# Moving element-wise sums from GpSimd to VectorE and giving the scatters a queue of their own, in a spectral filter followed by an eight-expert layer

## The chip, the core and the metric

The kernel runs on one core of a Trainium2 chip. The core has five engines, each with an instruction queue of its own that is worked off strictly in order: TensorE (PE in the profile; its weight loads are PEld), VectorE (DVE), ScalarE (ACT), GpSimd (POOL) and SyncE (SP, which here only issues DMA transfers). An instruction that must wait for another engine holds everything behind it in its own queue. The metric is the device time of one execution in microseconds (us). Nine executions of the kernel before gave a median of 1690.8 us (1688.98 to 1697.55).

## What is computed

Eight sequences of 2496 tokens with 256 channels are filtered in the frequency domain. Then each of the 19968 tokens goes to the one of eight experts for which its gate logit is largest, and the expert's output is scaled with the gate's probability.

```python
X = np.fft.rfft(x, axis=1)                      # x: (8, 2496, 256)
y = np.fft.irfft(X * (filt_r + 1j * filt_i)[None], n=2496, axis=1)
x = y.reshape(19968, 256)
logits = x @ w_gate                             # (19968, 8)
expert_idx = np.argmax(logits, axis=1)
gate_w = softmax(logits)[arange, expert_idx]
for e in range(8):                              # the rows of expert e
    h = np.maximum(x_e @ w1[e], 0.0)            # 256 -> 1024
    y_e = h @ w2[e]                             # 1024 -> 256
return gate_w[:, None] * y                      # float32 throughout
```

## The kernel before

**The filter, batch by batch.** The length 2496 = 39 x 64 is split into a 39-point and a 64-point transform, both done as matrix products, so that a batch goes through four stages: a (39 points, `stage_a`, L389), b (64 points and the filter, `stage_b`, L403), c (64 points back, `stage_c`, L432) and d (39 points back, `stage_d`, L451). Stages a and d run over six column chunks of four (the last of two) columns, b and c over five quarters of the frequencies. Between a and b, and between c and d, the data goes through DRAM (`zd`, `ud`), because rows and columns change places. All loads of x, z and u use one ring of seven buffers (`fin`). The first batch (`first_a`, `turn_z`, `first_c`, `turn_u`) stays on the chip.

Two kinds of sums concern us. `add_x` (L375) turns a chunk of x into sums `xs` (L382) and differences, written over the loaded tile (L383); stage a multiplies both. It runs on VectorE for batches 0 to 2 (`EARLY = 3`) and on GpSimd for batches 3 to 7. `xs` has two buffers. In `stage_b`, batches 0 to 2 keep the two products with the filter apart, and stage c accumulates both on TensorE. From batch 3 on, VectorE makes ys (L423), ScalarE copies the other parts in eight pieces of 32 partitions (L425), VectorE multiplies them (L426), and a sum of 128x1024 (L427) on GpSimd joins the two, for which stage c (L440) waits.

**Routing.** `turn_y` and `logits` make the gate logits; `route` (L569) then works on groups of eight columns (three groups per batch: 8, 8 and 6): some twenty small VectorE instructions find expert, gate and row for each token, with two small matrix products (L608, L609) for the ranks. Last, one indirect DMA per column, issued by GpSimd (L667, the "scatters"), writes 117 tokens to `rows`, a buffer in DRAM sorted by expert. The tiles `yo` that hold the tokens (six buffers) come free when their scatters have landed. `tile_map` (L685) works out which expert tiles a batch makes ready.

**The experts** run over tiles of 512, 256 or 128 rows: `rows_in` loads a tile (`xg`, by SyncE), `weights` loads w1 and w2, `turn_x` transposes (L798), `hidden` is the first product (L805) with a relu on ScalarE or VectorE, `result` the second (L819) with the gate, and GpSimd scatters the result to the output (L825).

**What sets the order.** The order of instructions on PE, DVE, ACT and SP is written by a loop at the end of the kernel (L988 to L1015). It takes steps from two lists: `STEPS` (the filter: fixed order, each with a TensorE cost) and `experts()`. Each turn of the loop emits one step, adds its TensorE cost to a planned clock `now`, and then calls `flush` (stores made in the turn before are issued), `more_loads` (fills the ring), up to four times `side`, and `prefetch` (rows and weights). A load counts as landed when `now` has passed its due time (`when`), 6 or 7 us after its issue. `free["v"]`, `free["s"]` and `free["p"]` are the planned times at which VectorE, ScalarE and GpSimd come free; `either` chooses by them whether VectorE or ScalarE copies a result out of PSUM.

`side` advances a queue `sides` of generators: `route` of each group of columns and, after a batch, `tile_map`. A generator is advanced one `yield` at a time, and the next one starts only when the one before has ended. The scatters are the last part of `route`; each `yield "pool"` stops the queue until GpSimd's planned time is within 1.5 us of `now`. Between the first part of `route` and its matrix products ten empty turns are let pass (L604). The count `held_y` of tiles in use falls by a group's tiles when its last scatter has been emitted; at six the filter's steps that need one are halted.

Of the kernel before, what the change touches and what calls it, by code (L numbers as in the profile page):

```python
# [14 lines left out]
ALU = mybir.AluOpType  # L15
# [21 lines left out]
NG = 2 * NI  # L37
# [117 lines left out]
def kernel(  # L155
# [18 lines left out]
    nc = tc.nc  # L174
# [94 lines left out]
    def pool(start, n):  # L269

        free["p"] = max(free["p"], start) + 1.3 * n
        return free["p"]
# [3 lines left out]
    EARLY = 3  # L276
# [98 lines left out]
    def add_x(b, c):  # L375

        m = CH[c][1] // 2
        xt = ins["x", b, c]
        xs = xss[b, c] = sb.tile([TP, 2, D], F32, tag="xs", name="xs", bufs=2)
        lo, hi_ = xt[:TP, :m], xt[:TP, m:2 * m]  # L380
        eng = nc.vector if b < EARLY else nc.gpsimd
        eng.tensor_tensor(xs[:, :m], lo, hi_, op=ALU.add)  # L382
        eng.tensor_tensor(hi_, lo, hi_, op=ALU.subtract)  # L383
        if b < EARLY:
            free["v"] = max(free["v"], now[0]) + 1.4
        else:
            free["p"] = max(free["p"], now[0]) + 2.6

    def stage_a(b, c):  # L389
        m = CH[c][1] // 2  # L390
# [12 lines left out]
    def stage_b(b, q):  # L403
        zi = outs.pop(("zi", q)) if b == 0 else ins.pop(("z", b, q))

        po = [bank(), bank()]
        for e in range(2):
            for o in range(2):
                rows = slice(o * HP, (o + 1) * HP)
                mm(po[o][e * HP:(e + 1) * HP, :], lhsT=tbs[rows, :], rhs=zi[rows, 2 * e:2 * e + 2, :], start=True, stop=True)  # L410

        ys = outs["y", b, q] = sb.tile([P, 2, 2 * D], F32, tag="ys", name="ys", bufs=2)
        yw = sb.tile([P, 2, 2 * D], F32, tag="yw", name="yw", bufs=2)
        if b < EARLY:

            for o in range(2):
                for y, h in ((ys, hr), (yw, hi)):
                    nc.vector.tensor_mul(y[:, o], po[o], h[:, q, 2 * o:2 * o + 2].rearrange("p j d -> p (j d)"))
            outs["w", b, q] = yw
            free["v"] = max(free["v"], now[0]) + 2.8  # L420
            return
        for o in range(2):
            nc.vector.tensor_mul(ys[:, o], po[o], hr[:, q, 2 * o:2 * o + 2].rearrange("p j d -> p (j d)"))  # L423
            for r in range(0, P, HB):
                nc.scalar.copy(out=yw[r:r + HB, o], in_=po[o][r ^ HB:(r ^ HB) + HB])  # L425
        nc.vector.tensor_mul(yw, yw, hi[:, q].rearrange("p (o j) d -> p o (j d)", o=2))  # L426
        nc.gpsimd.tensor_tensor(ys, ys, yw, op=ALU.add)  # L427
        free["s"] = max(free["s"], now[0]) + 4.7
        free["v"] = max(free["v"], now[0]) + 2.6
        free["p"] = max(free["p"], now[0]) + 2.5  # L430

    def stage_c(b, q):  # L432
        parts = [outs.pop((y, b, q)) for y in ("yw" if b < EARLY else "y")]
# [132 lines left out]
    scatters, rows_at, held_y = {}, {}, [0]  # L566


    def route(b, g):  # L569
        t0 = 8 * g  # L570
        w = min(8, NG - t0)
# [29 lines left out]
        nc.vector.tensor_reduce(sd, ex, axis=AX.X, op=ALU.add)  # L601
        yield

        for _ in range(10):  # L604
            yield
        rk = psr.tile([P, 2, E * NG], F32, tag="rk", name="rk")
        oef = oe.rearrange("p e t -> p (e t)")
        mm(rk[:TP, 0, :E * w], lhsT=tri, rhs=oef, start=True, stop=True)  # L608
# [7 lines left out]
        yos = [outs.pop(("o", b, c)) for c in range(2 * g, min(2 * g + 2, len(CH)))]  # L616
        for c, yo in enumerate(yos):
            n = min(4, w - 4 * c)
# [31 lines left out]
        rows = []  # L650
        for t in range(w):
            m = (HB - NB * (NI - 1)) * N1 if t0 + t >= NG - 2 else TP
            rows.append((row[:m, t:t + 1], yos[t // 4][:m, t % 4, :]))
        if b == B - 1 and t0 + w == NG:
# [8 lines left out]
            nc.vector.memset(fill.bitcast(I32)[:, D:D + 8], N)  # L663
            rows += [(pad[:, e:e + 1], fill) for e in range(E)]
        pool(now[0] + 2.0, 0)
        for t, (at, what) in enumerate(rows):
            sc = nc.gpsimd.indirect_dma_start(  # L667
                out=rowsd,
                out_offset=bass.IndirectOffsetOnAxis(ap=at, axis=0),
                in_=what,  # L670
                in_offset=None,
            )

            tc.declare_no_dep(sc.ins, group="scatter", reason="rows of their own")
            tc.declare_no_dep(sc.ins, group="listed", reason="rows of their own")
            tc.add_to_no_dep_group("scatter", sc.ins)
            scatters.setdefault(b, []).append(sc.ins.name)
            pool(now[0], 1)
            yield "pool"
        held_y[0] -= len(yos)  # L680
        if t0 + w == NG:
            rows_at[b] = free["p"] + 4.0


# [61 lines left out]
    work, idt, gts, xgs, xts, w1t, w2t, hs = [], {}, {}, {}, {}, {}, {}, {}  # L746
# [5 lines left out]
    late = {}  # L752

    def rows_in(i):

        n, e, r, b = work[i]
        r0 = nc.sync.value_load(r, min_val=0, max_val=TR - n * P)
        xg = xgs[i] = pools["moe"].tile([P, 4, DR], F32, tag="xg", name="xg")
        ld = nc.sync.dma_start(
            out=xg[:, :n], in_=rowsd[bass.ds(r0, n * P), :].rearrange("(p i) c -> p i c", i=n)  # L760
        )
        tc.add_to_no_dep_group("listed", ld.ins)
        for name in scatters.pop(b, ()):
# [68 lines left out]
        )  # L832


    sides = []

    def slot(k):

# [75 lines left out]
            if n:  # L914
                yield from tile_map(b, rows, n, rows == P)

    held = [None]

    def side():

        while sides and not (held[0] and free["p"] > now[0] + 1.5):
            try:
                held[0] = next(sides[0])

                free["v"] = max(free["v"], now[0]) + 0.3
                return
            except StopIteration:
                sides.pop(0)
                held[0] = None


    got = {"x": 0, "w1": 0, "w2": 0}
    used = {"x": 0, "w1": 0, "w2": 0}
    when = {}

    def prefetch():

        i = got["x"]
        if i < len(work) and rows_at[work[i][3]] <= now[0] and i - used["x"] < 2:
            rows_in(i)  # L940
            when["x", i] = now[0] + 6.0
            got["x"] += 1
        for what in ("w1", "w2"):
            h = got[what]
            if h < 2 * len(work) and rows_at[work[h // 2][3]] <= now[0] and (
                    h - used[what] < (3 if h < 2 * SHORT else 8)):
                weights(h, what == "w2")
                when[what, h] = now[0] + 7.0
                got[what] += 1
# [29 lines left out]
    with tc.manual_schedule(  # L979
        engines={mybir.EngineType.PE, mybir.EngineType.DVE, mybir.EngineType.Activation, mybir.EngineType.SP}  # L980
    ):
        nc.sync.dma_start(out=tas, in_=ta)
        more_loads()
        make_constants()
        fs, es = iter(STEPS), experts()
        credit = 0.0
        f, e = next(fs), next(es)
        while f or e:  # L988
            asked = e and e[2] in when

            halt = f and f[2] and f[2][0] in "uy" and held_y[0] == 6
            if e and asked and (not f and not sides or when[e[2]] <= now[0] and (credit > 0.0 or not f or halt)):
                e[0]()
                now[0] += e[1]
                credit -= e[1]
                e = next(es, None)
            elif f and not halt and (not f[2] or f[2] == "y" or f[2] in ins):
                f[1]()
                now[0] += f[3]
                credit = (credit if asked else 0.0) + share() * f[3]  # L1000
                left_t[0] -= f[3]
                f = next(fs, None)
            else:
                now[0] += 1.0
            flush()
            more_loads()
            for _ in range(4):
                side()
            if not f and not sides and not late:
                fft.close()  # L1010
                tail = ctx.enter_context(tc.tile_pool(name="tail", bufs=1))
                late["w1"] = ctx.enter_context(tc.tile_pool(name="w1b", bufs=8))
                late["n"] = 0
                late["w2s"] = tail.tile([P, E, FT, D], F32, name="w2s")
            prefetch()  # L1015
# [31 lines left out]
```

## Time and profile before

One profiled execution took 1690.43 us, of which 1688.7 us are its span (first to last instruction); 1.7 us lie around it.

| stretch of the span, us | PE busy | granted clock of PE | DVE busy | ACT busy | POOL busy | DMA share |
|---|---|---|---|---|---|---|
| 100 to 301.6 | 146.51 | 0.80 | 101.25 | 80.89 | 92.93 | 0.75 |
| 301.6 to 550 | 229.43 | 0.96 | 97.41 | 100.89 | 114.86 | 0.70 |
| 550 to 1200 | 627.95 | 0.99 | 161.75 | 215.16 | 195.29 | 0.48 |
| 1200 to 1689 | 482.50 | 0.99 | 20.68 | 150.26 | 68.50 | 0.51 |
| whole span | 1572.5 | 0.962 | 438.4 | 594.0 | 487.5 | |

The granted clock is the share of its full clock that TensorE got in the records of that stretch; a busy engine at a low clock does less. The DMA share is the mean busy share of the core's 16 DMA engines. At 301.6 us the first run of expert products without filter work between them begins; from about 1200 us on there are experts alone.

Instructions of the program as built, before and after, by engine: PE 4269 and 4269, DVE 1482 and 1532, ACT 1319 and 1354, POOL 458 and 373, SP 1928 and 1928.

### The profile page before, as it was taken

What the parts mean: (1) busy time and instruction counts of PE and PEld (TensorE: products, weight loads), DVE (VectorE), ACT (ScalarE), POOL (GpSimd) and SP (SyncE); (2) the same over time, 40 slices, a digit from 0 to 9 for tenths busy, and PEclk for the clock granted to TensorE, in tenths of its full rate; (3) what the DMA queues carried; (4) which work ended last, traced back from release to release, by engine and by line L of the source; (5) the groups of instructions that cost most, each with busy time, mean ns of one, the idle gap of its engine ahead of it and who ended that gap; (6) DMA issues with size and microseconds to landing.
All of it is one profiled execution on the core that took longest, in us unless ns stands there. A gap on an engine that the chain in (4) does not pass through costs nothing.

```text
span 1688.7 us, 22545 instructions
## 1 busy us (share of the span) xinstructions
PE 1572.5 (93%) x7218; PEld 1064.7 (63%) x7218; DVE 438.4 (26%) x1480; ACT 594.0 (35%) x1317; POOL 487.5 (29%) x453
## 2 busy tenths in 40 slices
PE   7987775899898999999979999999999999999998
PEld 5633442585444665557626666666666668889997
DVE  5564355124354115112244122112200000000000
ACT  4533444225453325232354323223222222333333
POOL 2034453442455235203234132133311111111111
PEclk9988786999999999999989999999999999999999
DMA  8579765578686357435374373343444446565661
GB/s 312 150 198 292 237 188 176 176 230 243 189 232 193 131 172 208 148 101 163 98 190 141 120 201 111 105 128 121 141 151 140 155 134 217 185 211 175 181 184 49
DMA packets 132325, 290.39 MB, mean 172 GB/s; under 512 B 21103, under 2 KB 62096, under 8 KB 132209
## 3 DMA queue, kind: packets, MB, share of 16 engines
q1 hardware_dynamic: 112993, 245.63, 48.5%
q0 software_dynamic: 19216, 43.33, 7.5%
q8 instruction: 59, 0.97, 0.2%
q14 instruction: 57, 0.47, 0.1%
HBM read 208.88 MB, written 80.90 MB: 172 GB/s over the span
## 4 chain that ended last, share of the span: by engine, by line
PE 82%; DVE 5%; issue 4%; DMA 3%; ACT 3%; POOL 2%; SPq 1%; POOLq 0%; DVEq 0%; ACTq 0%
PE bank L819 33%; PE bank L805 32%; PE bank L462 3%; PE bank L396 3%; ACT yw L425 2%; PE bank L798 2%; PE bank L410 2%; PE lt L551 2%; PE bank L537 1%; PE bank L440 1%; DMA fin<-in_x_dram 1%; PE bank L513 1%; POOL rows L667 1%; PE bank L489 1%; DMA xg<-rows 0%
## 5 line engine op out<-in xcount | busy, mean ns | idle before, releaser
L805 PE MATMUL bank<-xT,w1t 128*128 128x512 f32 (+2 forms) x2080 | 595.4, 440 | 14.0 <-issue 10.5
L819 PE MATMUL bank<-w2t,hT 128*128 128x256 f32 x2240 | 501.4, 382 | 5.7 <-issue 4.1
L805 PEld LDWEIGHTS bank<-xT,w1t 128*128 128x128 f32 x2080 | 340.6, 193 | 237.0 <-issue 203.2
L819 PEld LDWEIGHTS bank<-w2t,hT 128*128 128x128 f32 x2240 | 423.1, 191 | 74.6 <-issue 14.3
L825 POOL DMA_INDIRECT out_dram<-ys,idt x163 | 160.7, 986 | 773.6 <-ACT ys L824 443.9
L809 ACT ACTIVATE hT<-bank 128x512 f32<-128x512 f32 (+2 forms) x499 | 216.4, 435 | 327.4 <-PE bank L805 313.3
L667 POOL DMA_INDIRECT rows<-yo,row x176 | 177.6, 1009 | 236.1 <-DVE cnt L648 93.9
L824 ACT ACTIVATE ys<-bank,gts 128x256 f32<-128x256 f32 x156 | 73.6, 474 | 483.8 <-PE bank L819 420.0
L267 DVE COPY xT<-bank 128x512 f32<-128x512 f32 (+2 forms) x58 | 27.7, 477 | 540.0 <-PE bank L798 430.5
L425 ACT COPY yw<-bank 32x512 f32<-32x512 f32 x200 | 115.2, 576 | 52.3 <-DVE ys L423 41.7
L427 POOL TENSOR_TENSOR ys<-ys,yw 128x1024 f32<-128x1024 f32 x25 | 58.8, 2351 | 137.2 <-DVE yw L426 113.7
L819 PE MATMUL bank<-w2s,hT 128*128 x368 | 83.2, 379 | 0.0
L462 PE MATMUL bank<-fin,tds 120*117 120x512 f32 (+1 forms) x154 | 78.2, 627 | 1.3 <-ACT yw L425 1.3
L819 PEld LDWEIGHTS bank<-w2s,hT 128*128 128x128 f32 x368 | 68.1, 190 | 8.3
L396 PE MATMUL bank<-xs,tas 117*120 117x512 f32 (+1 forms) x84 | 45.2, 622 | 27.8 <-issue 12.3
L440 PE MATMUL bank<-ys,tcs 64*64 64x512 f32 x280 | 43.6, 676 | 17.5 <-POOL ys L427 17.4
L426 DVE TENSOR_TENSOR yw<-yw,hi 128x1024 f32<-128x1024 f32 x25 | 30.9, 1234 | 104.3 <-ACT yw L425 87.6
L466 DVE TENSOR_TENSOR yo<-bank,even 117x256 f32<-117x256 f32 x88 | 37.1, 422 | 78.5 <-ACT even L465 67.4
L537 PEld LDWEIGHTS bank<-ident,yo 117*128 117x128 f32 x352 | 40.5, 148 | 24.0 <-issue 16.7
L798 PEld LDWEIGHTS bank<-ident,xg 128*128 128x128 f32 x326 | 39.2, 143 | 23.0 <-issue 20.6
L537 PE MATMUL bank<-ident,yo 117*128 117x117 f32 x352 | 47.5, 278 | 6.2 <-ACT yw L425 2.8
L798 PE MATMUL bank<-ident,xg 128*128 128x128 f32 x326 | 47.4, 277 | 4.8 <-DMA xg<-rows 4.3
(140 smaller groups left out, 1105.2 us busy)
## 6 DMA issues: line engine op xcount, KB each, us to landing
w1t<-in_moe_w_dram SPq DMA_DIRECT2D x130, 512.0 KB
w2t<-in_moe_w_dram SPq DMA_DIRECT2D x84, 512.0 KB
fin<-in_x_dram SPq DMA_DIRECT2D x40, 512.0 KB
fin<-zd SPq DMA_DIRECT2D x140, 128.0 KB
ud<-uo SPq DMA_DIRECT2D x140, 128.0 KB
zd<-zo SPq DMA_DIRECT2D x70, 240.0 KB
fin<-ud SPq DMA_DIRECT2D x70, 240.0 KB
xg<-rows SPq DMA_DIRECT2D x28, 544.0 KB
```

The lines of the kernel that those rows point to most:

```text
L396: mm(p, lhsT=tas, rhs=v, start=True, stop=True)
L425: nc.scalar.copy(out=yw[r:r + HB, o], in_=po[o][r ^ HB:(r ^ HB) + HB])
L440: mm(pe[e][o * HP:(o + 1) * HP, :], lhsT=tcs[rows, o, i, :], rhs=y[rows, o, :], start=(i == 0), stop=(i == len(parts) - 1))
L462: mm(p[:TP, :], lhsT=tds[:k, :], rhs=uv[:, i], start=True, stop=True)
L537: nc.tensor.transpose(pt[:, 2 * i + dh, :TP], yo[:, j + i, dh * P:(dh + 1) * P], ident[:TP, :TP])
L667: sc = nc.gpsimd.indirect_dma_start(out=rowsd, out_offset=bass.IndirectOffsetOnAxis(ap=at, axis=0), in_=what, in_offset=None,)
L798: nc.tensor.transpose(pt[:, j, :], xg[:, j, dh * P:(dh + 1) * P], ident)
L805: mm(p[:, :m], lhsT=w1t[2 * i + k // FH2][:, dh, k % FH2 * P:(k % FH2 + 1) * P], rhs=xts[i][:, dh, :m], start=(dh == 0), stop=(dh == DH - 1))
L809: lambda: nc.scalar.activation(hT[:, :m], p[:, :m], AF.Relu))
L819: mm(p[:, :D], lhsT=hs[i][k][:, j * P:(j + 1) * P], rhs=w2, start=(k == 0), stop=(k == FT - 1))
L824: lambda: nc.scalar.activation(ys, p[:, :D], AF.Copy, scale=gate))
L825: nc.gpsimd.indirect_dma_start(out=out, out_offset=bass.IndirectOffsetOnAxis(ap=idt[i].bitcast(U32)[:, j, :], axis=0), in_=ys, in_offset=None,
```

## The change

1. `add_x` and the sum in `stage_b` run on VectorE in all batches. GpSimd keeps the scatters (and the constants at the start).
2. The scatters leave `route` for a generator of their own, `scatter`, in a queue `scats` beside `sides`; `scatter_on` advances it once per turn while GpSimd's planned time is within 1.5 us. The next group's routing need not wait for the scatters of the group before. `held_y` falls tile by tile, with every fourth scatter.
3. `side` takes a step whenever VectorE's planned time is at most 1 us ahead of `now`, and books 0.45 us for it (0.3 before). The ten empty turns become six that are marked "wait" and book nothing.
4. After each step the planned clock `now` is moved up to at least 3 us before VectorE's and ScalarE's planned times. `prefetch` counts a batch's rows as not ready (`rows_at.get`) while its scatters are still to be emitted.

```diff
 def add_x(b, c):
-        eng = nc.vector if b < EARLY else nc.gpsimd
-        eng.tensor_tensor(xs[:, :m], lo, hi_, op=ALU.add)
-        eng.tensor_tensor(hi_, lo, hi_, op=ALU.subtract)
-        if b < EARLY:
-            free["v"] = max(free["v"], now[0]) + 1.4
-        else:
-            free["p"] = max(free["p"], now[0]) + 2.6
+        nc.vector.tensor_tensor(xs[:, :m], lo, hi_, op=ALU.add)
+        nc.vector.tensor_tensor(hi_, lo, hi_, op=ALU.subtract)
+        free["v"] = max(free["v"], now[0]) + 1.4
 def stage_b(b, q):
-        nc.gpsimd.tensor_tensor(ys, ys, yw, op=ALU.add)
+        nc.vector.tensor_tensor(ys, ys, yw, op=ALU.add)
-        free["v"] = max(free["v"], now[0]) + 2.6
-        free["p"] = max(free["p"], now[0]) + 2.5
+        free["v"] = max(free["v"], now[0]) + 3.9
 def route(b, g):
-        for _ in range(10):
-            yield
+        for _ in range(6):
+            yield "wait"
...
         pool(now[0] + 2.0, 0)
+        scats.append(scatter(b, rows, len(yos), t0 + w == NG))
+
+    def scatter(b, rows, n, last):
         for t, (at, what) in enumerate(rows):
             sc = nc.gpsimd.indirect_dma_start(
...
             pool(now[0], 1)
-            yield "pool"
-        held_y[0] -= len(yos)
-        if t0 + w == NG:
+            if t % 4 == 3 and t // 4 < n or t == len(rows) - 1 and n > len(rows) // 4:
+                held_y[0] -= 1
+            yield
+        if last:
             rows_at[b] = free["p"] + 4.0
 def side():
-        while sides and not (held[0] and free["p"] > now[0] + 1.5):
+        while sides and free["v"] <= now[0] + 1.0:
             try:
-                held[0] = next(sides[0])
-                free["v"] = max(free["v"], now[0]) + 0.3
+                if next(sides[0]) != "wait":
+                    free["v"] = max(free["v"], now[0]) + 0.45
                 return
...
+    def scatter_on():
+        while scats and free["p"] <= now[0] + 1.5:
+            try:
+                next(scats[0])
+            except StopIteration:
+                scats.pop(0)
 def prefetch():
-        if i < len(work) and rows_at[work[i][3]] <= now[0] and i - used["x"] < 2:
+        if i < len(work) and rows_at.get(work[i][3], now[0] + 1.0) <= now[0] and i - used["x"] < 2:
...
 # the loop that writes the order
+            now[0] = max(now[0], free["v"] - 3.0, free["s"] - 3.0)
             flush()
             more_loads()
             for _ in range(4):
                 side()
+            scatter_on()
```

More of the change, by code (lines that the diff above doesn't have):

```diff
@@ L832, in result @@
         )
-    sides = []
+    sides, scats = [], []
     def slot(k):
@@ L915, in after @@
                 yield from tile_map(b, rows, n, rows == P)
-    held = [None]
     def side():
-        while sides and not (held[0] and free["p"] > now[0] + 1.5):
+        while sides and free["v"] <= now[0] + 1.0:
             try:
-                held[0] = next(sides[0])
-                free["v"] = max(free["v"], now[0]) + 0.3
+                if next(sides[0]) != "wait":
+                    free["v"] = max(free["v"], now[0]) + 0.45
                 return
@@ L928, in side @@
                 sides.pop(0)
-                held[0] = None
+    def scatter_on():
[4 more added lines that the diff above has]
+                scats.pop(0)
     got = {"x": 0, "w1": 0, "w2": 0}
@@ L944, in prefetch @@
             h = got[what]
-            if h < 2 * len(work) and rows_at[work[h // 2][3]] <= now[0] and (
+            if h < 2 * len(work) and rows_at.get(work[h // 2][3], now[0] + 1.0) <= now[0] and (
                     h - used[what] < (3 if h < 2 * SHORT else 8)):
@@ L991 @@
             halt = f and f[2] and f[2][0] in "uy" and held_y[0] == 6
-            if e and asked and (not f and not sides or when[e[2]] <= now[0] and (credit > 0.0 or not f or halt)):
+            if e and asked and (not f and not sides and not scats or when[e[2]] <= now[0] and (credit > 0.0 or not f or halt)):
                 e[0]()
@@ L1008 @@
                 side()
-            if not f and not sides and not late:
+            scatter_on()
+            if not f and not sides and not scats and not late:
                 fft.close()
```

## The prediction

> **What bounds the kernel now.** I read the page first, then busy times by stretch, then the waits of TensorE, and last the timelines of PE, GpSimd and VectorE around the longest waits.
>
> ```profile
> PE 82%; DVE 5%; issue 4%; DMA 3%; ACT 3%; POOL 2%; SPq 1%; POOLq 0%; DVEq 0%; ACTq 0%
> 100.00:301.60 201.60, 146.51 (x691) 69.31 (x690) 101.25 (x328) 80.89 (x173) 92.93 (x81) 0.80 0.75 227
> 301.60:550.00 248.40, 229.43 (x997) 145.10 (x998) 97.41 (x320) 100.89 (x216) 114.86 (x97) 0.96 0.70 209
> ```
>
> TensorE makes 82% of the chain that ended last, so the time is TensorE's work plus what it loses. The two other lines (columns: stretch, its length, busy PE, PEld, DVE, ACT, POOL, granted clock, DMA share, GB/s) show where it loses. In the first stretch it is idle for 201.6 - 146.5 = 55 us and runs at 0.80 of its clock, which costs 146.5 x 0.20 = 29 us more: 84 us. In the second it is 19 us idle and 229.4 x 0.04 = 9 us to the clock: 28 us. From 550 to 1200 it is 22 us idle, and from 1200 us on nothing but the kernel's last microseconds is lost. What the change can win lies before 1200 us, most of it before 301.6. There no engine is full (DVE 50%, ACT 40%, POOL 46%) and the DMA share is 0.75: the stretch is bound by waits for one another. Three places show GpSimd's part in them.
>
> ```profile
> 130.72 0.98 POOL L667 DMA_INDIRECT rows<-yo,row  x1 [0.30 <-issue]
> 131.72 1.27 POOL L382 TENSOR_TENSOR xs<-fin 117x512 f32<-117x512 f32 x1
> ...
> 240.45 0.99 POOL L667 DMA_INDIRECT rows<-yo,row  x1 [0.30 <-issue]
> 241.46 1.27 POOL L382 TENSOR_TENSOR xs<-fin 117x512 f32<-117x512 f32 x1
> ```
>
> ```profile
> 133.05 2.06 PE L396 MATMUL bank<-xs,tas 117*120 117x512 f32 x2 [8.82 <-issue]
> 168.41 0.69 PE L396 MATMUL bank<-xs,tas 117*120 117x256 f32 x2 [3.48 <-issue]
> 242.78 2.06 PE L396 MATMUL bank<-xs,tas 117*120 117x512 f32 x2 [3.69 <-POOL xs L382]
> ```
>
> The last number in brackets is the engine's idle time before the row. Each of these stage-a products starts within 0.1 us of the end of an `xs` sum on GpSimd (131.72 + 1.27 = 132.99; 241.46 + 1.27 = 242.73), and each sum starts as the last of six or eight scatters before it ends. The sums stood behind scatters, and the scatters behind routing. The first two waits are named "issue", but the times give GpSimd.
>
> ```profile
> 260.47 2.35 POOL L427 TENSOR_TENSOR ys<-ys,yw 128x1024 f32<-128x1024 f32 x1
> ...
> 260.56 2.27 DVE L692 TENSOR_SCALAR av_i<-av_i 1x8 int32<-1x8 int32 x1
> 262.87 1.19 DVE L696 CAST av<-av_i 1x8 f32<-1x8 int32 x1
> 264.18 1.22 DVE L701 TENSOR_TENSOR base<-done,eoff 1x8 f32<-1x8 f32 x1
> ```
>
> VectorE instructions on eight elements, 0.16 us elsewhere, last until GpSimd's sum is over. Taking every form's median over the whole timeline, 27 VectorE instructions are stretched in this way, by 30 us in all, 10.6 of them from 100 to 301.6 us, nearly all beside a GpSimd sum.
>
> **The sums change engine.** GpSimd loses 25 full and 5 half pairs of `add_x` and 25 of the L427 sums. On VectorE a full pair costs 0.71 + 0.69 = 1.40 us and a half pair 0.42 + 0.43 = 0.85 (the rows of batches 0 to 2), against 2.58 and 1.49 on GpSimd; an L427 sum has the shape of L426, 1.23 us, against 2.35. VectorE gets 25 x 1.40 + 5 x 0.85 + 25 x 1.23 = 70 us and gets back up to 30 us of stretching. Of this, 11 full and 2 half pairs and 5 sums fell between 100 and 301.6 us: 15.4 + 1.7 + 6.2 = 23.3 us, less 10.6. In the built order the planner also gives ScalarE 18 copies, 13 relus and 4 gates that VectorE had.
>
> First stretch, gains:
> - The three waits behind scatters, 16.0 us. Bounds 0 and 16.0, since something else may be late next: behind the first stands a stage-d product (140.80) for which u is loaded only from 130.44 on; behind the second, VectorE's L466 (169.67) waits 4.67 us for a scatter to free a `yo`. I take 7.5, half.
> - The stretched instructions: 4.8 us at 260 to 265 lie on the chain of waits (PE then idles 8.65 us to 274.67). Bounds 0 and 10.6; I take 4.8.
> - L427 shorter: PE waited 1.5 us for it here; 1.2 of its time goes (2.35 - 1.23), and I take 1.2, from bounds 0 and 1.5.
>
> **What the order does to the loads.** No DMA is added or taken out; 1,928 SP instructions stand in both programs. But they move. I counted the TensorE work (at full clock, from rows of the chain: 32 halves of L805 in 13.73 us, 64 of L819 in 13.81) between a load's place in the program and its first reader. Between work 101 and 158, which is this stretch, the x loads had 1, 0, 5, 3, 4, 1, 2 and 1 us of work to land in; now 6, 3, 8, 7, 12, 8, 8 and 2. The z and u loads gain less. An x load takes 6.55 and 7.78 us where the chain of waits runs through it (120.98 and 141.13): 14.3 us. Bounds 0 and 14.3; with some 5 us more lead each, I take 8.
>
> SP's queue holds the stores of z and u before these loads, and they wait for the same copies as before. Scatters and output stores on GpSimd now pass no sums; scatters land sooner after routing, which frees `yo` sooner and is in the 7.5. Routing keeps its instructions; the rank products (L608) of groups 5 to 9 stand at TensorE work 115, 136, 171, 184 and 203 instead of 132, 139, 152, 177 and 204, some earlier, some later: 0.
>
> **The clock.** It stood at 0.80 where PE idled 27% of the time (first stretch) and at 0.96 where it idled 8%. The idle gains so far are 7.5 + 4.8 + 1.2 + 8 = 21.5 us; idle then is 33.5 of some 169 us, 20%, and on the line between the two rows the clock is 0.86. The work, 146.5 x 0.80 = 117 us, then takes 136 us instead of 146.5: 10.5, from bounds 0 (the clock stays) and 23 (all gains at their upper ends, 42 us: idle 9%, clock 0.95).
>
> First stretch, costs:
> - VectorE's extra work, 12.7 us net; bounds 0 and 12.7. VectorE makes 13% of the chain in this stretch (24.4 of the 193.6 us of its pieces); 13% of 23.3 is 3, which I take. The cover is VectorE's own idle time, 100 us of 201.6, mostly waits for PE and ScalarE.
> - The head of the queue. On GpSimd the `xs` sums waited 9.5 us for x and 4.7 for PE (two buffers). On VectorE such a wait holds the filter products, stage d's sums and routing, and TensorE waits for these. Bounds 0 and 14.2; with the earlier loads I take 3.
>
> Sum: 21.5 + 10.5 - 6 = 26 us.
>
> **301.6 to 1200 us.** PE waits for L427 three times, 15.9 us (9.93 the longest); each ends 1.2 us sooner: 3.6. Stretched instructions: 19.7 us here, of which I take 2, from bounds 0 and 5.8, PE's waits for the VectorE lines L597 and L466. VectorE gains 46.7 - 19.7 = 27 us of work at 29% busy; I take 2 lost, bounds 0 and 27 (a cover wholly gone). ScalarE gets 18 x 0.59 + 13 x 0.44 + 4 x 0.47 = 18 us; PE waits some 25 us for ScalarE in all, 36% busy; 2 lost, bounds 0 and 18. The order also spreads the experts: before, work 165 to 225 was almost pure experts and the next filter batch came after it; now filter and experts alternate from 125 to 350, but work 276 to 328 carries 27 us of filter, where VectorE is needed most. I price that at 0, bounds -10 and +10. Sum: +2. From work 950 on TensorE's order is the same in both: 489 us, unchanged.
>
> **A rule against it.** VectorE's sums read two operands from SBUF. The Trainium skill, "SBUF — State Buffer", section "SBUF: two separate sides", says that such an instruction and a GpSimd instruction that reads SBUF exclude each other for their whole length on a shared port. It agrees with the stretched rows above, but it also speaks against the change: the scatters would now be held by 85 more VectorE sums. In the trace a scatter takes 0.99 us, and only 5 of 176 took over 1.4. By the rule at its worst, each sum blocking a scatter once, that is 70 us on GpSimd; GpSimd is freed of 131 us of sums, so even then it ends ahead.
>
> **Forecast and rivals.** 1690.4 - 26 - 2 = 1662 us, 1647 to 1676: half way to the DMA floor below and half way to no change. The profiled execution lies 0.4 us under the median, which changes nothing.
> - *The DMA floor (faster).* If alternating experts fill every gap, the first stretch shrinks to its transfers: 201.6 x 0.75 = 151 us, as from 283 to 300 us the share was full (1.02). That wins 50, with 8 more later: 1632. Against it: latencies, not shares, ended the waits.
> - *Loads are late next.* The waits behind scatters are replaced by waits for u and z, as the chain has it between 117 and 149 us: 7.5 becomes 1.5, 8 becomes 0, the clock gives 4; 1.5 + 4.8 + 1.2 + 4 - 6 + 2 = 7.5: 1683 (1676 to 1693).
> - *VectorE's queue (slower).* The sums stand ahead of filter products and stage-d sums and hold them while they wait for x and for `xs` buffers. Price: 14.2 + 12.7 in the first stretch, 7.6 of such waits later (21.8 in all less 14.2), and a third of the 27 us, 9: 43.5. Without the clock's gain, 21.5 + 5.6 remain: 16 slower, 1707 (1693 to 1725). It decides once the waits and work on VectorE's path exceed some 27 us. For it: PE already waits on VectorE and ScalarE in these stretches. Against: VectorE is half idle, and batches 0 to 2 do these sums on it with waits of only 4.6 us (2.7 for x, 1.9 for PE).
>
> Chances: forecast 0.47, DMA floor 0.15, loads 0.17, VectorE's queue 0.21. About 0.2% (3.4 us) can be told from no change; 0.06 of the loads case lies within that. Faster 0.73, same 0.06, slower 0.21. The range runs from the DMA floor's neighbourhood to the near part of the slower case: 1636 to 1700 leaves out about 0.07 and 0.13.
>
> **What would show it.** Right: no sums on GpSimd; from 100 to 301.6 us of old time PE idles some 20 us less and its clock is near 0.86; no eight-element VectorE instruction of 1 to 2 us; the first dense experts some 25 us earlier. Wrong: L418, L423 or L466 waiting behind L382 for x or PE; PE's waits unchanged but named z, u or weights; more idle time between 400 and 600 us, where the filter is now denser.

## The result and the profile after

The changed kernel takes 1727.64 us (median of 10 runs, 1724.44 to 1736.12) against 1694.54 us for the kernel before on the same chip (31 runs). The ratio is 1.0207, 95% interval 1.019 to 1.0224: it is slower by 2.1%. The forecast was 1662 us, the range 1636 to 1700. The profiled execution has a span of 1732.5 us, 43.8 more than that of before, and a mean granted clock of 0.952 (0.962 before). The medians differ by 33.1 us only: the profiled execution after is one of the longer ones and that of before one of the shorter, so some 10 us of what the two profiles differ in changes from execution to execution.

The chain of waits of the profile after can be followed back only to 589 us, so I compare the busy times by stretch. First the two stretches of the prediction, after the change (columns: stretch, its length, busy PE, PEld, DVE, ACT and POOL with instructions, granted clock, DMA share, GB/s):

```profile
100.00:301.60 201.60, 145.35 (x691) 67.50 (x685) 105.68 (x311) 84.81 (x177) 46.42 (x46) 0.83 0.74 215
301.60:550.00 248.40, 203.96 (x853) 129.09 (x854) 101.38 (x348) 102.71 (x221) 58.22 (x58) 0.87 0.65 194
```

In the first, PE is idle for 56.3 us (55.1 before): no idle time was won where I expected 21.5 us. In the second its idle time went from 19.0 to 44.4 us and its clock from 0.96 to 0.87. Idle time and clock together (busy x (1 - clock)) cost 44.4 + 26.5 = 71 us there, against 28 before. These 43 us are about the whole difference of the two spans. For the experiments I use round stretches; here the kernel before and the changed one:

```profile
0.00:300.00 300.00, 232.57 (x1248) 127.51 (x1248) 157.06 (x450) 127.58 (x265) 107.41 (x105) 0.86 0.73 224
300.00:600.00 300.00, 279.44 (x1196) 179.51 (x1197) 105.90 (x341) 115.65 (x245) 126.21 (x107) 0.96 0.66 197
600.00:1200.00 600.00, 577.95 (x2356) 365.31 (x2354) 154.74 (x571) 200.50 (x397) 185.37 (x172) 0.99 0.48 142
```

```profile
0.00:300.00 300.00, 232.40 (x1240) 126.19 (x1240) 163.75 (x435) 130.57 (x267) 58.04 (x67) 0.88 0.71 214
300.00:600.00 300.00, 252.40 (x1055) 160.69 (x1056) 112.87 (x380) 119.18 (x253) 71.07 (x71) 0.89 0.63 190
600.00:1200.00 600.00, 580.45 (x2343) 363.66 (x2342) 146.53 (x510) 207.10 (x407) 135.68 (x136) 0.98 0.47 140
```

Lost to idle time and clock, in us, from such lines (the last two rows were profiled on a chip on which the kernel before takes some 20 us less, so up to about 20 us of what they gain on the first two is the chip's):

| kernel | 0 to 300 | 300 to 600 | 600 to 1200 | sum |
|---|---|---|---|---|
| before | 100 | 32 | 28 | 160 |
| after | 95 | 75 | 31 | 202 |
| after, xs sums earlier (0.983, below) | 65 | 15 | 33 | 113 |
| xs sums on GpSimd, filter block split (0.965, below) | 58 | 13 | 14 | 85 |

The name of the new wait stands at the top of PE's waits (columns: engine and tile, line, what it waited for, us in all, times, longest). After:

```profile
PE bank L392 <- DVE xs L381: 68.6, 18, 7.2
PE rk L603 <- DVE oe L592: 8.7, 2, 5.8
PE bank L435 <- DVE ys L423: 8.4, 1, 8.4
```

L392 is stage a (L396 before), L381 the `xs` sum (L382 before). In the kernel before, all of stage a's waits for `xs`, named or read as "issue", came to some 23 us (12.3 + 7.3 + 3.7). 28.6 of the 68.6 us lie in the first stretch, where they took the place of the waits behind scatters (16.0 us); 28.9 lie in the second, where before had none. One of them, on VectorE and then on PE (start, duration, engine, line, tiles; in brackets the idle time before, and its cause):

```profile
294.01 1.28 DVE L419 TENSOR_TENSOR ys<-bank,hr 128x512 f32<-128x512 f32 x2
299.47 1.23 DVE L422 TENSOR_TENSOR yw<-yw,hi 128x1024 f32<-128x1024 f32 x1 [4.18 <-ACT yw L421]
300.73 1.22 DVE L423 TENSOR_TENSOR ys<-ys,yw 128x1024 f32<-128x1024 f32 x1
301.87 0.68 DVE L381 TENSOR_TENSOR xs<-fin 117x512 f32<-117x512 f32 x1
302.59 0.69 DVE L382 TENSOR_TENSOR fin<-fin 117x512 f32<-117x512 f32 x1
303.20 0.15 DVE L695 CAST av<-av_i 1x8 f32<-1x8 int32 x1
```

```profile
302.70 2.03 PE L392 MATMUL bank<-xs,tas 117*120 117x512 f32 x2 [7.24 <-DVE xs L381]
```

The `xs` sum needs 0.68 us, and its row shows no wait for x, whose load was issued at 276.4. It stands in VectorE's queue behind the filter block: two products, 4.18 us of waiting for ScalarE's eight copies, a multiply and a sum. Between the end of L419 (295.29) and the start of the `xs` sum (301.87) lie 6.6 us, and PE idles 7.24. Of the longer waits for L381, eight with 44 us in all stand right behind L422 and L423 like this; the other four of over 3 us (18.3 us) stand behind routing's small instructions and stage d's sums. The wait inside the block is in VectorE's list for both kernels, before and after:

```profile
DVE yw L426 <- ACT yw L425: 87.6, 21, 4.2
```

```profile
DVE yw L422 <- ACT yw L421: 100.2, 24, 4.2
```

The last DVE line above (L695, a cast of eight elements in 0.15 us, 1.19 before) shows that what I expected of the stretched instructions did happen: over the whole timeline they fell from 27 with 30.3 us to 9 with 4.7 us (3.2 of these beside sums that GpSimd still makes for the constants at the start).

### The profile page after: what moved, and what is told of

Its sections match the earlier page's. It is cut to its first block, busy times and chain, and to the rows that moved or that the text cites. A ratio compares the mean times of both kernels' runs of the same rounds, so it can differ in the third digit from the quotient of the medians.

```text
span 1732.5 us, 22447 instructions
## 1 busy us (share of the span) xinstructions
PE 1588.3 (92%) x7218; PEld 1072.4 (62%) x7218; DVE 458.0 (26%) x1530; ACT 615.1 (36%) x1352; POOL 357.1 (21%) x368
## 4 chain that ended last, share of the span: by engine, by line
PE 61%; issue 1%; DVE 1%; ACT 1%; DMA 1%; SPq 0%; another core or an unknown queue 0%; POOLq 0%; DVEq 0%; ACTq 0%
PE bank L818 28%; PE bank L804 27%; PE bank L797 2%; PE bank L457 1%; ACT yw L421 1%; PE bank L532 1%; PE bank L392 1%; PE lt L546 1%; PE bank L435 0%; PE bank L406 0%; DVE yw L422 0%; DMA fin<-zd 0%; DMA ud<-uo 0%; PE bank L557 0%; PE rk L604 0%
## 5 line engine op out<-in xcount | busy, mean ns | idle before, releaser
L808 ACT ACTIVATE hT<-bank 128x512 f32<-128x512 f32 (+2 forms) x512 | 222.8, 438 | 317.7 <-PE bank L804 295.4
L392 PE MATMUL bank<-xs,tas 117*120 117x512 f32 (+1 forms) x84 | 55.3, 747 | 74.1 <-DVE xs L381 68.6
L457 PE MATMUL bank<-fin,tds 120*117 120x512 f32 (+1 forms) x154 | 87.0, 688 | 7.6 <-ACT yw L421 3.9
L267 ACT COPY zo<-bank 120x512 f32<-120x512 f32 (+1 forms) x79 | 42.9, 553 | 94.2 <-PE bank L392 82.0
L392 PEld LDWEIGHTS bank<-xs,tas 117*120 117x120 f32 x84 | 15.5, 223 | 95.5 <-issue 78.9
L457 PEld LDWEIGHTS bank<-fin,tds 120*117 120x117 f32 (+1 forms) x154 | 30.9, 212 | 51.7 <-issue 37.7
L422 DVE TENSOR_TENSOR yw<-yw,hi 128x1024 f32<-128x1024 f32 x25 | 30.6, 1226 | 104.3 <-ACT yw L421 100.2
L392 PE MATMUL bank<-fin,tas 117*120 117x512 f32 (+1 forms) x84 | 51.8, 706 | 0.3 <-PE bank L392 0.3
```

The source lines that it names most:

```text
L267: either(n, lambda: nc.vector.tensor_copy(o, i), lambda: nc.scalar.copy(out=o, in_=i))
L392: mm(p, lhsT=tas, rhs=v, start=True, stop=True)
L457: mm(p[:TP, :], lhsT=tds[:k, :], rhs=uv[:, i], start=True, stop=True)
L808: lambda: nc.scalar.activation(hT[:, :m], p[:, :m], AF.Relu))
```

## The experiments

The expectations speak of three theories. A, the place in the queue: TensorE waits for sums that stand behind other VectorE work. B, the amount: VectorE's longer work costs, wherever it stands. C, the order: the queue of the scatters, routing's pacing and the planned clock (parts 2 to 4 of the change) cost. The experiments ran on five chips; the kernel before took 1674 us on two of them and 1693 to 1696 on three. So times are compared as ratios to the kernel before on the same chip. The first four expectations give times for a chip on which it takes 1694.5 us: 1685 is a ratio of 0.994, 1708 of 1.008, 1720 of 1.015, 1730 of 1.021.

### Undoing one part, or doing one alone

The first puts the pairs of `add_x` back on GpSimd for batches 3 to 7, and keeps the rest of the change:

```diff
-        nc.vector.tensor_tensor(xs[:, :m], lo, hi_, op=ALU.add)
-        nc.vector.tensor_tensor(hi_, lo, hi_, op=ALU.subtract)
+        eng = nc.vector if b < EARLY else nc.gpsimd
+        eng.tensor_tensor(xs[:, :m], lo, hi_, op=ALU.add)
+        eng.tensor_tensor(hi_, lo, hi_, op=ALU.subtract)
...
```

> The changed kernel with one part undone: the xs sums and differences of batches 3 to 7 run on GpSimd again; the sum in stage b stays on VectorE, scatter queue and pacing stay as changed. Theory A (place in the queue: on VectorE the xs sums stand behind the filter product that waits 4.2 us for ScalarE's eight copies, and TensorE waits for them, 68.6 us in 18 waits): those waits go, stage a's waits for sums fall under 20 us, time 1685 to 1700. Theory B (amount: 70 us more work on VectorE, of which this takes back 39): about 1708. Theory C (order: scatter queue, pacing and planned clock spoil the mix of filter and experts): stays at 1720 to 1730.

Measured: 0.9974 (0.9951 to 0.9997). The second puts the sum of `stage_b` back instead:

```diff
-        nc.vector.tensor_tensor(ys, ys, yw, op=ALU.add)
+        nc.gpsimd.tensor_tensor(ys, ys, yw, op=ALU.add)
...
```

> The changed kernel with the other part undone: the 128x1024 sum of stage b runs on GpSimd again, the xs sums stay on VectorE. Theory A: the xs sums still stand behind the 4.2 us wait, only 1.2 us of what is ahead of them goes in some 14 places: 1708 to 1720, waits of stage a for VectorE still over 45 us. Theory B: 31 of 70 us taken back, about 1712, waits not told. Theory C: 1720 to 1730.

Measured: 1.0264 (1.0234 to 1.0293), above what any of the three theories gave, though PE's waits for `xs` stay, as theory A has it (82.2 us in 21). The third has both edits, that is parts 2 to 4 of the change alone:

> Both kinds of sums on GpSimd as before; the scatter queue, routing's pacing and the planned clock as changed: parts 2 to 4 of the change alone. Theories A and B: the loss is gone, 1680 to 1697 (the earlier loads may even win). Theory C: the loss is here, 1720 to 1730.

Measured: 0.999 (0.9972 to 1.0008). The fourth is the kernel before with part 1 alone (both kinds of sums on VectorE):

> The kernel before with both kinds of sums on VectorE and nothing else changed: part 1 alone. Theory A: stage a's products wait for VectorE some 60 us in all, 1715 to 1735. Theory B: the same time, with the waits spread over all VectorE lines. Theory C: 1685 to 1697.

Measured: 1.0218 (1.0188 to 1.0247). The loss is in `add_x` on VectorE, with the order of before around it and with that of after; theory C falls. (Each of these edits also shifts the written order, since the planner books the sums' time.) PE's waits in the last one and in the first:

```profile
PE bank L392 <- DVE xs L381: 64.8, 18, 7.2
```

```profile
PE rk L607 <- DVE oe L596: 16.7, 4, 5.0
PE bank L396 <- POOL xs L382: 6.5, 2, 4.6
```

The wait for `xs` comes and goes with the engine of `add_x`. The stage-b sum on VectorE is a small gain at most: 0.9974 against 0.999, whose intervals overlap, and 1.0207 against 1.0264, on different chips.

### Moving the sums, or the block in front of them

Earlier place, the same work on VectorE:

```diff
+                early = at - 0.05
+                if k > 0:
+                    early = min(early, int(max(at - 0.001, 0.0) * (NQ + 1)) / (NQ + 1) - 0.001)
-                steps.append((at - 0.05, lambda c=c: add_x(k + 1, c), ("x", k + 1, c), 0.0))
+                steps.append((early, lambda c=c: add_x(k + 1, c), ("x", k + 1, c), 0.0))
```

> The changed kernel with each pair of xs sums of batches 3 to 7 planned ahead of the filter block that precedes its stage-a product instead of directly ahead of that product; they stay on VectorE, so VectorE has the same work. Theory A (place in the queue: the sums stand behind the filter block's 4.2 us wait for ScalarE and its 2.4 us of multiply and sum): PE's waits for VectorE's xs sum fall from 68.6 us to under 25, and the ratio to the kernel before falls from 1.021 to 1.000 or below. Theory B (the amount of VectorE work): nothing is taken off VectorE, the ratio stays within 1.015 to 1.025, and PE's waits move to other VectorE instructions. Theory D (the sums only block something else when they come early: they wait for x loads or for a free xs buffer at the head of the queue, and hold the filter products): waits of VectorE's xs sum for DMA or PE grow above 20 us, ratio 1.01 to 1.03.

Measured: 0.9832 (0.9813 to 0.9852). PE's waits, and the first stretch of the prediction:

```profile
PE bank L435 <- DVE ys L423: 9.3, 2, 7.8
PE bank L392 <- DVE xs L381: 5.1, 4, 2.2
```

```profile
100.00:301.60 201.60, 167.98 (x792) 79.63 (x786) 127.89 (x414) 98.15 (x210) 57.71 (x57) 0.91 0.88 265
```

68.6 us of waiting became 5.1, and the first stretch has the idle time that I had forecast: 33.6 us (worked out as 33.5), at a clock of 0.91 (0.86). That the two agree so closely is luck: this is another kernel, on a chip on which before is 20 us faster. Theory D, that early sums block others, falls: VectorE's `xs` sums waited 3.1 us for x and 1.9 for PE. Next, the filter block is cut in two:

```diff
...
+        outs["w", b, q] = yw
+    def stage_b2(b, q):
+        ys, yw = outs["y", b, q], outs.pop(("w", b, q))
         nc.vector.tensor_mul(yw, yw, hi[:, q].rearrange("p (o j) d -> p o (j d)", o=2))
         nc.vector.tensor_tensor(ys, ys, yw, op=ALU.add)
...
+                if q < NQ and k >= EARLY:
+                    steps.append((at + 0.1, lambda q=q: stage_b2(k, q), None, 0.0))
```

> The changed kernel with the second half of the filter block (the multiply of yw and the sum of ys and yw) made a step of its own, planned half a filter step later, so that VectorE takes up other work, the xs sums among it, while ScalarE copies. The same instructions on every engine. Theory A: PE's waits for VectorE's xs sum fall under 25 us; the ratio falls to 1.005 or below, if stage c doesn't come to wait for the later sum instead. Theory B: the ratio stays within 1.015 to 1.025.

Measured: 0.9858 (0.9836 to 0.9881), with 33.1 us of PE waits for `xs` left, 8 more than expected. Both edits together:

> Both edits of the two runs before at once. Theory A: PE waits under 15 us for the xs sums, ratio 0.985 to 1.000; if it is no better than the early sums alone, the split brings nothing once the sums are out of the way. Theory B: 1.015 to 1.025.

Measured: 0.9838 (0.981 to 0.9865), no better than either: PE's waits for `xs` fell to 2.8 us, but stage c now waited 19.0 us in 7 for the later stage-b sum. Then the split with `add_x` on GpSimd:

> The split of the filter block with the xs sums on GpSimd (the kernel that measured 0.997, plus the split). A control of the split: by theory A nothing that TensorE waits for stands behind the filter block any more, so the split moves the time by less than 0.5% (0.992 to 1.002). If the split by itself is worth over 1%, the 4.2 us wait held more than the xs sums (routing, stage d's sums), and the split kernel with sums on VectorE must be compared with this one instead.

Measured: 0.9651 (0.963 to 0.9671), far outside the expectation for a control. VectorE's wait for the copies fell to 10.5 us in 4 (104.6 in 25 in the same kernel without the split), and 600 to 1200 us lost 14 us instead of 27. PE's waits for routing (`oe`) fell from 16.7 to 3.7 us, and those of expert products for VectorE's copy of their rows (`xT`) from 10.8 us to none. So the block held more than the `xs` sums. I took that to hold for every kernel:

> The kernel before with nothing but the split of the filter block (the multiply of yw on VectorE and the sum of ys and yw on GpSimd become a step of their own, half a filter step later). Theory A in its wider form (VectorE's in-order wait of 4.2 us for ScalarE's copies holds whatever is queued behind it: the xs sums in the changed kernel, routing and stage d's sums in every kernel): the split by itself is worth 2 to 3.5% here too, ratio 0.965 to 0.98. Rival (the split pays only because the xs sums or the scatter queue and pacing of the change are there): ratio 0.99 to 1.00.

> Parts 2 to 4 of the change (scatter queue, pacing by VectorE's count, planned clock) with the split, both kinds of sums on GpSimd. It differs from the run before only in parts 2 to 4, and from the 0.965 kernel only in the engine of the sum of ys and yw. If parts 2 to 4 are worth something once the filter block no longer holds VectorE's queue, this lies at least 0.5% under the split of the kernel before; if they are worth nothing, as without the split (0.999), the two agree within 0.4%. If the sum on VectorE is worth something, this lies above 0.965 by 0.3 to 1%.

Measured: 0.9943 (0.9917 to 0.9969) for the kernel before with the split, 0.9945 (0.9922 to 0.9969) with parts 2 to 4 as well. That widening was wrong. PE's waits in the two:

```profile
PE bank L445 <- POOL ys L433: 41.5, 9, 12.3
```

```profile
PE bank L445 <- POOL ys L433: 47.8, 10, 13.2
```

With the multiply later, the stage-b sum on GpSimd comes later still, at times behind scatters, the experts' output scatters and `xs` sums, and stage c waits for it. In the 0.965 kernel the same sum on VectorE leaves 16.4 us in 4:

```profile
PE bank L444 <- DVE ys L433: 16.4, 4, 7.8
PE bank L396 <- POOL xs L382: 5.6, 3, 2.6
```

So the stage-b sum on VectorE is worth 0.2 to 0.6% without the split and 3% with it (0.9651 against 0.9945, on two chips). I read this as two waits of which each hides behind the other. Two variants of the 0.965 kernel, the `xs` sums on GpSimd planned early, and the second half of the block at half the distance (`at + 0.05`):

> The 0.965 kernel (xs sums on GpSimd, sum of ys and yw on VectorE, split) with the xs sums planned ahead of the preceding filter block. PE still waits 5.6 us for xs on GpSimd there; expected 0.96 to 0.967 if that wait goes and nothing else moves. If early sums hold GpSimd's queue (scatters behind a wait for x or for an xs buffer), 0.967 to 0.98.

> The 0.965 kernel with the second half of the filter block planned a quarter of a filter step after the first half instead of half a step (0.05 instead of 0.1 of a slot). If the gain comes from the copies (4.7 us) being over when VectorE reaches the multiply, a quarter of a step (some 10 us of TensorE work) is long enough, and the ratio stays within 0.96 to 0.97; if it needs the whole distance, it rises to 0.975 or more.

Measured: 0.9647 (0.9598 to 0.9696), no different; and 0.9766 (0.9718 to 0.9814), so the distance matters. Why it does is not settled, as the order around the block differs too.

### Is it the place or the amount?

In the split kernels the `xs` sums on VectorE cost 2% (0.9858 against 0.9651). PE's waits for them, 33.1 us against 5.6, could be most of it; but with the sums early as well, when only 2.8 us of these waits are left, the ratio is still 0.9838, so the place of the sums alone doesn't explain it. I added work that nobody reads where the changed kernel has these sums:

```diff
...
+            free["v"] = max(free["v"], now[0]) + 1.4
+            for n in (8, 8, 4) if CH[c][1] == 4 else (8, 4):
+                dum = sb.tile([TP, 8], F32, tag="dum", name="dum", bufs=1)
+                two = hr[:TP, 0].rearrange("p j (g d) -> p (j g) d", d=64)
+                nc.vector.tensor_reduce(out=dum[:, :n], in_=two[:, :n], op=ALU.max, axis=AX.X)
```

> The changed kernel with the xs sums of batches 3 to 7 on GpSimd (that kernel measured 0.997), plus VectorE work that nobody reads, at the places where the changed kernel has its sums there: three reductions (two of 117x512, one of 117x256, two of them for a half pair) per pair of sums, 1.4 us planned. What it computes is thrown away. Theory B (the amount): VectorE is as full as in the changed kernel, so the ratio is 1.015 to 1.025. Theory A (TensorE waits for the sums): 0.995 to 1.005; the stretching by GpSimd's sums is there as in the 0.997 kernel.

> The 0.965 kernel with the same unread VectorE work. If the 2% between the two split kernels (0.965 with the xs sums on GpSimd, 0.986 with them on VectorE) is the amount of work, the ratio is 0.98 to 0.99; if it is that TensorE waits for these sums in VectorE's queue, it stays at 0.962 to 0.970.

Measured: 1.0086 (1.0057 to 1.0115) and 0.9809 (0.9782 to 0.9836). The first lies between the theories; the second is what B expected. The line of the added work in the first (shortest, median and longest in ns):

```profile
L392 DVE TENSOR_REDUCE dum<-hr x85: 420/676/687, 121.8 to 726.2; 117x8 f32<-117x512 f32 x55, 117x4 f32<-117x256 f32 x30
```

That is 55 x 0.676 + 30 x 0.42 = 49.8 us, more than the 25 x 1.40 + 5 x 0.85 = 39.3 us of the sums. The first line shown of the diff also changes the written order, since the planner books the time. The next four take the two apart:

> The changed kernel with the xs sums of batches 3 to 7 on GpSimd (0.997), and 1.4 us booked on VectorE in the planner for each pair, with no work behind it. If the order that the booking makes is what costs (theory C in a new form), the ratio is 1.005 to 1.012; if VectorE's time does, it is 0.994 to 1.001.

> The 0.997 kernel with the unread VectorE work (49.8 us in 85 reductions in the profile of the run before, where the sums would be 39.3) but without the booking, so all other instructions stand in the order of the 0.997 kernel. If VectorE's time costs (theory B): 1.005 to 1.012; if the order does: 0.996 to 1.002.

> The 0.965 kernel with the booking and no work behind it. Order: 0.978 to 0.984; VectorE's time: 0.962 to 0.969.

> The 0.965 kernel with the unread work and no booking. VectorE's time: 0.975 to 0.984; order: 0.964 to 0.970.

| `add_x` on GpSimd | without the split | with the split |
|---|---|---|
| nothing added | 0.9974 (0.9951 to 0.9997) | 0.9651 (0.963 to 0.9671) |
| booking alone | 0.992 (0.9892 to 0.9948) | 0.9686 (0.9656 to 0.9716) |
| work alone | 1.0212 (1.0182 to 1.0243) | 0.9732 (0.9691 to 0.9772) |
| both | 1.0086 (1.0057 to 1.0115) | 0.9809 (0.9782 to 0.9836) |

Of the last four expectations one held (0.9686 for the booking with the split). The booking without the split came out below both ranges, the work without the split above both, and the work with the split between the two. The two rows in the middle share a chip; the others were measured on other chips.

Within a column, kernels with the same booking have the same instruction order on TensorE, ScalarE and SyncE, and on VectorE but for the added rows. So 49.8 us of unread VectorE work cost 2.4 and 1.7% without the split (some 40 and 28 us) and 0.8 and 1.2% with it (14 and 21 us). The booking's order gives -0.5 and +0.4%, hardly more than the intervals. The kernel with the work alone, without the split, by stretch:

```profile
0.00:300.00 300.00, 230.61 (x1248) 125.26 (x1248) 182.44 (x492) 125.82 (x261) 93.08 (x98) 0.89 0.72 220
300.00:600.00 300.00, 261.60 (x1069) 162.05 (x1070) 123.28 (x355) 113.43 (x240) 100.73 (x96) 0.94 0.63 190
```

From 0 to 600 us PE is busy for 492 us, against 524 in the same kernel without the work (240.97 + 282.58; on a chip on which before is 20 us faster) and 516 with the booking alone (232.88 + 282.85; on the chip of this run), though VectorE is busy for only 306 of these 600 us, 51%. The longest wait of an expert product shows what comes later (VectorE's rows and, last, PE's):

```profile
202.59 1.85 DVE L391 TENSOR_REDUCE dum<-hr 117x8 f32<-117x512 f32 x3
204.35 1.28 DVE L427 TENSOR_TENSOR ys<-bank,hr 128x512 f32<-128x512 f32 x2
209.81 1.23 DVE L430 TENSOR_TENSOR yw<-yw,hi 128x1024 f32<-128x1024 f32 x1 [4.17 <-ACT yw L429]
211.06 1.22 DVE L431 TENSOR_TENSOR ys<-ys,yw 128x1024 f32<-128x1024 f32 x1
...
212.35 0.74 DVE L267 COPY xT<-bank 128x256 f32<-128x256 f32 x2
```

```profile
212.87 1.62 PE L812 MATMUL bank<-xT,w1t 128*128 128x256 f32 x3 [16.82 <-DVE xT L267]
```

The copy of the expert's rows stands behind the unread work and the filter block; the same product waits 9.17 us without that work. So A and B were no alternatives. At this place of VectorE's queue, time itself costs, though no product reads its result: what stands behind it in the queue comes later, and TensorE with it. The early placement shows that the same sums need not cost anything elsewhere in the queue. How the changed kernel's 2.3% (0.9974 to 1.0207) divide into VectorE's time and TensorE's waiting for the sums themselves stays open; unread work at the early place was not tried, the early placement also changes the order of the expert products around it, and no kernel with added work has the changed kernel's order.

## Why the prediction was wrong

The step that failed is the costs on VectorE, "the head of the queue" (3 us) and "VectorE's extra work" (3 and 2 us), and with it the choice among the cases. I asked what the `xs` sums would hold up in VectorE's queue, and not what would hold up the sums: PE waited 68.6 us for them.

- **The head of the queue: 3 us, bounds 0 and 14.2.** I priced it by what the `xs` sums themselves waited for on GpSimd, x (9.5) and PE (4.7). That wait hardly occurred: on VectorE they waited 2.5 us for x and 2.7 for PE, all in the first batch. What they stand behind was left out. PE's waits for them are 28.6 us in the first stretch alone and 68.6 in all, beyond the upper bound. The row was in the trace of before: 87.6 us in 21 waits for ScalarE's copies, 4.2 each.
- **VectorE's extra work: 3 of 12.7 and 2 of 27, covered by "VectorE's own idle time, mostly waits for PE and ScalarE".** That cover does not exist for an instruction queued behind such a wait. Unread work of 49.8 us cost 28 to 40 us, 0.6 to 0.8 of its length. For the 39.7 us of the two upper bounds together that makes an estimate of 22 to 32 us, not 5.
- **The waits behind scatters: 7.5 us of 16.0.** They went, and the waits for VectorE's `xs` took their place. "Something else may be late next" was right; I named u and `yo`, and it was the moved sum.
- **Stretched instructions and the shorter sum.** Right: 25.6 of 30.3 us of stretching gone; PE's waits for the stage-b sum fell from 17.4 us in 4 to 8.4 in one. As a gain in time, the stage-b sum on VectorE is worth 0.2 to 0.6%, with both effects in it.
- **Loads 8 us and clock 10.5.** The clock rose by itself, from 0.80 to 0.83, though idle time stayed. A gain from the loads isn't seen in the changed kernel, nor as time in parts 2 to 4 alone (0.999). With the sums earlier, idle time reached what was worked out and the clock more (33.6 us; 0.91), but no run tells the loads' part in it from the rest.
- **301.6 to 1200 us: +2.** It lost 43 us from 301.6 to 550. The sign that I listed under "what would show it", more idle time between 400 and 600 us, is there: 27.7 us, 17.4 before. The other, L418, L423 or L466 waiting behind the sums for x or PE, hardly is (5.2 us in the first batch).
- **The order of the experts and parts 2 to 4: 0.** As a sum it held: 0.999.
- **The rule of the Trainium skill** ("SBUF — State Buffer", section "SBUF: two separate sides"), at its worst each VectorE sum holding a scatter, 70 us. The trace agrees that they are held, and shows how little it costs: 4.1 us in all after the change and 4.4 before (rows in the last section), where the held scatters were those beside L426 and the sums of batches 0 to 2. Of the three stretched rows that I took to agree with the rule, L692 and L696 read one operand; what I told of the rule speaks of two.
- **The rival "VectorE's queue", 1707 us (0.21), had the sign, the right queue and half of the mechanism**, and too small a price. Half of it had the sums wait at the head for x and for `xs` buffers and hold the filter products; the runs showed the reverse, the sums held by the filter block. The other half, VectorE's longer work (12.7 and 9 us), the unread work bears out in kind. My argument against it, that batches 0 to 2 do these sums on VectorE with waits of only 4.6 us, failed on a difference visible in the code: there stage b is four products straight from PSUM (L414 in the kernel after), with no wait for ScalarE's copies.

## What to carry to other kernels

An operation moved to another engine's queue starts after everything in front of it there, so price it by the rows that will stand before it, waits included, and not by that engine's busy share: a 4.2 us wait inside a block is idle time in the profile and no room for the work behind it. Before a move, cut such a block at its wait and let other work fill it; then try each engine again, because the gains of the two edits need not add (here the split alone gave 0.6%, the stage-b sum on VectorE alone at most 0.3 to 0.6%, and the two together, with parts 2 to 4, 3.5%). Where a planner writes the order, add unread work with and without its booking to tell the cost of time from the cost of order.

## What the runs showed of the hardware

Small VectorE instructions that lasted 0.7 to 3.2 us beside GpSimd's sums disappear with these sums: some 30 us of stretching in 27 instructions before, 22 to 23 with only the stage-b sum off GpSimd, 3 to 5 with none left there but those at the start. It is worth little in this kernel: taking the stage-b sum off GpSimd gave 0.2 to 0.6% by itself.

The hold works the other way too. In the profile after, ten of GpSimd's 347 indirect DMAs (scatters and output) began while VectorE was in an `xs` sum or difference, a stage-b sum or the product before it, and each ended 0.8 to 0.9 us after that instruction did. The 329 that met none of these took 0.99 us in the mean and 1.02 at most. One of the ten, and the product that it met:

```profile
199.69 1.95 POOL L665 DMA_INDIRECT rows<-yo,row  x1 [0.30 <-issue]
```

```profile
199.56 1.23 DVE L422 TENSOR_TENSOR yw<-yw,hi 128x1024 f32<-128x1024 f32 x1 [4.04 <-issue]
```

TensorE's granted clock went with its idle time from 300 to 600 us: it was 0.89 where PE was busy 252 us, 0.96 at 279 and 0.99 at 290, and between before and after 27.0 us less busy time there came with 43.7 us more loss. In the first 300 us it is not so simple: kernels in which PE was busy 231 to 233 us had clocks from 0.86 to 0.90.
